# Keys and queries with the dimensions in rows, values by units and weights by chunks: a layout change of the inputs in a fused attention and feed-forward kernel

## The chip, the core and the metric

The kernel runs on one core of one Trainium2 chip, in float32. The metric is device time in microseconds (us) of one launch. Five engines work side by side: PE (TensorE, matmuls), DVE (VectorE), ACT (ScalarE), POOL (GpSimd) and SP (SyncE, which here only issues DMAs). PE reads its operands from SBUF, on-chip memory of 128 partitions, and writes its results to PSUM, from where ACT or DVE must fetch them. Inputs lie in HBM and are brought to SBUF by 16 DMA engines that all queues share.

## The reference

For 2 batches of 8 heads, 768 positions and 64 dimensions: attention of each query over the keys less than 16 positions away, and over 24 summary keys (the maximum of each block of 32 keys) with the mean values of those blocks; then two feed-forward layers on the 1536 resulting rows of 512.

```python
k_sum = k.reshape(B, H, nb, 32, D).max(axis=3)
v_sum = v.reshape(B, H, nb, 32, D).mean(axis=3)
scores_l = np.where(abs(pos_q - pos_k) < 16, scale * q @ k.T, -1e9)
scores_s = scale * q @ k_sum.T + np.log(32)
a = softmax(concat[scores_l, scores_s])
x = a @ concat[v, v_sum]                       # then rows of 512: 8 heads x 64
x = (silu(x @ w_gate) * (x @ w_val)) @ w_out   # 512 -> 1536 -> 512
h = x @ w_in                                   # 512 -> 2048
out = (h * clip(h + 3, 0, 6) / 6) @ w_out2     # 2048 -> 512
```

The feed-forward weights come as 64-bit floats and are turned into pairs of 32-bit parts on the chip (`weights`, L360): four DVE instructions on the bits, one or two on ACT, and a subtraction.

## The kernel before

The 1536 rows are cut into four token blocks t of 384 (two for each batch b), the eight heads into four pairs c. `attention` (L790) adds, for one block, the work of its four pairs: `keys` and `values` for the first block of a batch, then `queries`, `scores`, `sums`, `norm`, `head`, `outputs`.

A matmul contracts over partitions. For the scores it needs keys and queries with the 2 x 64 dimensions of a pair in the partitions, but the inputs have positions in rows. So `load_rows` (L551) brings 128 positions to the partitions, 64 floats (256 bytes) at a time, `rows` (L590) turns them with three transposing matmuls against the identity (L592), and `put` copies the result out of PSUM into `kT` or `qT` (`copy`, L271, so that the trace shows L273, L275 or L277). The query's copy multiplies by -1/8. For batch 0 the rows lie in room of the later tiles x2 and x3 (`stage`, L558; tiles named early in the trace), for batch 1 in rings of four (`kn`) and two (`qn`). There is one `kT` for each pair, used by both batches in turn, with 16 positions of zeros at either end. `ksum` is the maximum of each 32 columns of `kT` (L621).

`scores` (L677) multiplies 64 queries with the 24 summary keys and with a window of 96 keys (L697). `sums` (L709) adds the mask and takes the negated maximum in one DVE instruction (L717), then ACT exponentiates (L724). `head` (L741) divides by the sum on POOL or DVE and transposes the weights (L754), `outputs` (L760) multiplies them with `vw`, a tile with 24 rows of mean values and a window of 96 values for each of the block's six units of 64 queries (L768). The windows overlap, and `load_vw` (L577) fetches them in three DMAs for each pair and block, from rows of 64 floats; it must wait until the weighting of the block before has read the tile.

The feed-forward part takes three matmuls (L334 to L336) for each product of split numbers. Its first group of columns is woven with the attention of the later blocks. Weights of `w_gate`, `w_val` and `w_in` are fetched by columns in pieces of 128 64-bit numbers (1 KB), those of the two output matrices in rows of 4 KB (`w_src`, L353).

A planner (`Plan`, L94 to L255) sets the order of all engines' queues: each step is added with a rank and an assumed time for each engine that could do it; the planner runs the steps through a model of the engines and rings, six times with new ranks, and keeps the best order. All loads count as one engine "dma" there and, but for the second pair's first keys and queries (ACT's queue, `second`, L565), are issued by SP in that order. Where the plan leaves PE idle, `fill` puts up to ten matmuls of zeros (L835).

Of the kernel before, what the change touches and what calls it, by code (L numbers as in the profile page):

```python
# [34 lines left out]
NEG = 1.0e9  # L35

# [23 lines left out]
def consts():  # L60

    import numpy as np

    a = np.zeros((P, P + 3 * NK + NS), np.float32)
    a[:, :P] = np.eye(P, dtype=np.float32)
    i = (np.arange(P) % QB)[:, None]
    second = (np.arange(P) >= QB)[:, None]
    w = np.arange(NW)[None, :]
    near = np.abs(i - (w - HALO)) < WIN
    for n in range(3):  # L70
        m = a[:, P + n * NK : P + (n + 1) * NK]
        inside = second | (w >= HALO) if n == 0 else ~second | (w < QB + HALO) if n == 2 else (w >= 0)
        m[:, :NS] = -np.log(np.float32(BLOCK))
        m[:, NS:] = np.where(near & inside, 0.0, NEG)
    p = np.arange(WP)
    a[p, P + 3 * NK + p * (S // WP) // BLOCK] = 1.0 / BLOCK
    return a

# [180 lines left out]
def tile_kernel(ctx: ExitStack, tc: tile.TileContext, q, k, v, w_gate, w_val, w_out1, w_in2, w_out2, cst, out):  # L259
# [30 lines left out]
    for n in ("kn", "qn", "v3", "qT", "p", "st", "pt"):  # L290
        pools[n] = ab_p
# [61 lines left out]
    def w_src(layer, i, f):  # L353
        if layer == 0 and i < 2 or layer == 1 and i == 0:
            w = ((w_gate, w_val), (w_in2,))[layer][i]
            return w[:, f * P : (f + 1) * P].bitcast(U32).rearrange("(c p) f -> p c f", p=P)
        w = (w_out1, w_out2)[layer]
        return w[f * P : (f + 1) * P, :].bitcast(U32)

    def weights(rank, layer, g, i, f, after):  # L360
# [4 lines left out]
        def load():  # L365
            src = w_src(layer, i, g * (G1, G2)[layer] + f)
            dst = new(raw, [P, 512, 2], U32).rearrange("p a b -> p (a b)")
            if len(src.shape) == 3:
                dst = dst.rearrange("p (c f) -> p c f", c=KC)
            nc.sync.dma_start(out=dst, in_=src)  # L370
# [175 lines left out]
    kT = [ap_.tile([P, S + 2 * HALO], F32, name=f"kT{c}") for c in range(NP)]  # L546
    vw = [ap_.tile([P, NB, P], F32, name=f"vw{c}") for c in range(NP)]
# [3 lines left out]
    def load_rows(dst, src, queue=nc.sync):  # L551

        for h in range(2):
            queue.dma_start(out=dst[:, :, h * D : (h + 1) * D], in_=src[h].rearrange("(r p) d -> p r d", p=P))

    early = {}

    def stage(kind, c, part):  # L558

        x = 3 if kind == "k" else 2  # L560
        if x not in early:
            early[x] = xpool.tile([P, 8, TR, P], F32, tag=f"x{x}", name=f"early{x}")
        return early[x][:, 2 * c + part]
# [13 lines left out]
    def load_vw(t, c):  # L577
        b, s0 = divmod(t * T, S)
        va = v[b, 2 * c]
        end, cut0, cut1 = (0, HALO, NW) if s0 == 0 else (NB - 1, 0, QB + HALO)  # L580
        inner = 1 if s0 == 0 else 0
        first = s0 + end * QB - HALO + cut0
        src = bass.AP(va.tensor, va.offset + first * D, [[D, cut1 - cut0], [S * D, 2], [1, D]])
        nc.sync.dma_start(out=vw[c][NS + cut0 : NS + cut1, end, :].rearrange("p (h d) -> p h d", h=2), in_=src)
        for h in range(2):
            first = h * S + s0 + inner * QB - HALO
            src = bass.AP(va.tensor, va.offset + first * D, [[D, NW], [QB * D, NB - 1], [1, D]])
            nc.sync.dma_start(out=vw[c][NS : NS + NW, inner : inner + NB - 1, h * D : (h + 1) * D], in_=src)

    def rows(ps, src):  # L590
        for r in range(TR):
            nc.tensor.transpose(ps[:, r, :], src[:, r, :], ident)  # L592

    def keys(rank, b, c):

        for part in range(2):
            n = ("kn" if b else "k0", b, c, part)

            def load(n=n, part=part):
                if b == 0:  # L600
                    tiles[n] = stage("k", c, part)
                else:
                    new(n, [P, TR, P])
                load_rows(tiles[n], k[b, 2 * c : 2 * c + 2, part * T : (part + 1) * T], second(b, c))

            add(rank - LEAD["k_load"], {"dma": 1.05}, load, w=[n])
            ps = prep_bank(b, "k", b, c, part)

            def turn(n=n, ps=ps):
                tiles[ps] = new_bank(ps, [P, TR, P])  # L610
                rows(tiles[ps], tiles[n])

            def put(e, part=part, ps=ps):
                dst = kT[c][:, HALO + part * T : HALO + (part + 1) * T].rearrange("q (r p) -> q r p", p=P)
                copy(e, dst, tiles[ps])

            add(rank, {"pe": 0.3}, turn, r=[n, ("cs",)], w=[ps, ("kT", c)])
            add(rank - LEAD["k_put"], {"act": 0.4, "dve": 0.47}, put, r=[ps], w=[("kT", c)])

        def most():  # L620
            nc.vector.tensor_reduce(  # L621
                ksum[c], kT[c][:, HALO : HALO + S].rearrange("q (n i) -> q n i", i=BLOCK), AX.X, ALU.max
            )

        add(rank, {"dve": 0.87}, most, r=[("kT", c)], w=[("ksum", c)])
# [27 lines left out]
    def queries(rank, t, c):  # L653
        n, ps, qt = ("qn" if t > 1 else "q0", t, c), prep_bank(t, "q", t, c), ("qT", t, c)
        b, s0 = divmod(t * T, S)

        def load():
            if t < 2:
                tiles[n] = stage("q", c, t)
            else:  # L660
                new(n, [P, TR, P])
            load_rows(tiles[n], q[b, 2 * c : 2 * c + 2, s0 : s0 + T], second(t, c))

        add(rank - LEAD["q_load"], {"dma": 1.05}, load, w=[n])

        def turn():
            tiles[ps] = new_bank(ps, [P, TR, P])
            new(qt, [P, TR, P])
            rows(tiles[ps], tiles[n])

        def put(e):
            copy(e, tiles[qt], tiles[ps], -1.0 / float(D) ** 0.5)

        add(rank, {"pe": 0.3}, turn, r=[n, ("cs",)], w=[ps, qt])
        add(rank - LEAD["q_put"], {"act": 0.4, "dve": 0.47}, put, r=[ps], w=[qt])

    def scores(rank, t, c):  # L677

        half, qt = t % 2, ("qT", t, c)
        names = [(t, c, h) for h in range(2)]  # L680

        def go(j):
            if j == 0:
                new(("st", t, c), [P, 4, 2 * TR])
            for x in names:
                if j == 0:
                    tiles["at", "s", *x] = new_bank(("at", "s", *x), [P, TR, NK])
                    new(("p", *x), [P, TR, NK])
            q2 = tiles[qt].rearrange("q r p -> q (r p)")
            for far in (True, False):  # L690
                for a in range(2):
                    for h in range(2):
                        hs, u = slice(h * D, (h + 1) * D), 2 * j + a
                        k0 = half * T + u * QB
                        rhs = ksum[c][hs, :] if far else kT[c][hs, k0 : k0 + NW]
                        cols = slice(0, NS) if far else slice(NS, NK)
                        nc.tensor.matmul(  # L697
                            tiles["at", "s", *names[h]][a * QB : (a + 1) * QB, j, cols],
                            lhsT=q2[hs, u * QB : (u + 1) * QB], rhs=rhs, start=True, stop=True,
                        )  # L700

        for j in range(TR):
            add(rank, {"pe": 0.37}, lambda j=j: go(j), r=[("kT", c), ("ksum", c), qt],
                w=[("st", t, c)] + [(n, *m, *x) for x in names for n, *m in (("at", "s"), ("p",))] if j == 0 else
                [("at", "s", *x) for x in names])
# [3 lines left out]
    def sums(rank, t, c, h):  # L709
# [5 lines left out]
        def top(r):  # L715
# [3 lines left out]
                scale=1.0, scalar=3.0e38, op0=ALU.add, op1=ALU.min, accum_out=tiles[st][:, 0, h * TR + r : h * TR + r + 1],  # L719
# [94 lines left out]
    def clear():  # L814
        for c in range(NP):
            nc.gpsimd.memset(kT[c][:, :HALO], 0.0)
            nc.gpsimd.memset(kT[c][:, HALO + S :], 0.0)
        for c in range(NP):
            nc.gpsimd.memset(vw[c], 0.0)

    add(-50.0, {"pool": 3.2}, clear, w=[(n, c) for c in range(NP) for n in ("kT", "vw", "vs")])
# [93 lines left out]
_INS = ["q", "k", "v", "moe_w_gate", "moe_w_val", "moe_w_out", "moe2_w_in", "moe2_w_out"]  # L915
# [20 lines left out]
```

## Time and profile before

| | |
|---|---|
| median of three runs | 653.56 us (653.07 to 653.57) |
| profiled execution | 654.63 us, span 652.9 us |
| PE busy | 640.2 us of the span |
| DVE, ACT, POOL busy | 438.3, 289.7, 52.9 us |
| DMA packets | 73319, of them 45744 under 512 bytes |

The span runs from the first to the last instruction of the profiled execution. A PE that is busy may be at work on fill matmuls, so its share alone says nothing of useful work. Rows of the trace give a start, a duration, the engine, the line and what is written from what.

### The profile page before, as it was taken

Reading aid. Unit: us, or ns where it says so; the run is one execution under the profiler, and the core shown is the slowest. Engines: PE = TensorE matmul, PEld = TensorE weight load, DVE = VectorE, ACT = ScalarE, POOL = GpSimd, SP = SyncE. Lnnn points to the kernel's source line nnn. Section 1 sums busy time; section 2 is a strip of 40 time slices with the busy share of each in tenths; the row PEclk is TensorE's granted clock in tenths of the full one; section 3 lists DMA queues with packets and bytes.
Section 4 is the critical chain, followed back from the end, with each engine's and each line's share of the span. In section 5 each row is a group of like instructions: output and inputs, shape, how many; then the busy total and the mean of one; then the engine's idle time right before and its main releaser. Section 6 shows DMA issues by size and latency. Waiting matters only on the chain.

```text
span 652.9 us, 11688 instructions
## 1 busy us (share of the span) xinstructions
PE 640.2 (98%) x4576; PEld 601.1 (92%) x4576; DVE 438.3 (67%) x972; ACT 289.7 (44%) x674; POOL 52.9 (8%) x73
## 2 busy tenths in 40 slices
PE   7799999999999999999999999999999999999997
PEld 6688888999999999999999999999999999999996
DVE  3789974589997978369754997286738753333332
ACT  3788788455543433134322564354424332222220
POOL 3435443100000000000000000000000000000000
PEclk9989999999999999999999999999999999999999
DMA  8998944043433233003210133012301000000112
GB/s 185 220 225 232 193 85 140 1 130 132 159 130 98 97 97 97 1 27 103 81 50 0 66 103 124 1 65 64 131 1 40 25 1 0 2 1 0 50 49 96
DMA packets 73319, 53.84 MB, mean 82 GB/s; under 512 B 45744, under 2 KB 66736, under 8 KB 73264
## 3 DMA queue, kind: packets, MB, share of 16 engines
q1 hardware_dynamic: 70864, 52.51, 28.7%
q10 hardware_dynamic: 2400, 0.59, 0.6%
q8 instruction: 36, 0.59, 0.4%
q14 instruction: 19, 0.16, 0.1%
HBM read 49.94 MB, written 3.15 MB: 81 GB/s over the span
## 4 chain that ended last, share of the span: by engine, by line
PE 92%; DMA 4%; ACT 2%; issue 0%; SPq 0%; DVE 0%; POOL 0%; ACTq 0%; POOLq 0%
PE mm L334 16%; PE mm L335 15%; PE mm L336 15%; PE mmb L334 13%; PE mmb L335 13%; PE mmb L336 13%; PE at_s L697 2%; PE pv L768 2%; DMA vn<-in_v 2%; DMA early<-in_k 1%; PE at_t L754 1%; ACT p L724 1%; DMA kn<-in_k 1%; PE pv L835 1%; PE at_q L592 1%
## 5 line engine op out<-in xcount | busy, mean ns | idle before, releaser
L334 PE MATMUL mm<-x,wa 128*128 128x384 f32 x196 | 69.2, 353 | 0.0
L336 PE MATMUL mm<-x,wa 128*128 128x384 f32 x196 | 65.9, 336 | 0.0
L335 PE MATMUL mm<-x,wa 128*128 128x384 f32 x196 | 65.9, 336 | 0.0
L387 ACT ACTIVATE raw<-raw 128x512 f32<-128x512 f32 x68 | 46.2, 680 | 26.3 <-DVE bits L379 23.4
L335 PE MATMUL mmb<-x,wb 128*128 128x384 f32 x160 | 53.5, 335 | 0.0
L335 PE MATMUL mm<-x,wb 128*128 128x384 f32 x160 | 53.5, 335 | 0.0
L336 PE MATMUL mmb<-x,wb 128*128 128x384 f32 x160 | 53.5, 334 | 0.0
L336 PE MATMUL mm<-x,wb 128*128 128x384 f32 x160 | 53.5, 334 | 0.0
L334 PE MATMUL mm<-x,wb 128*128 128x384 f32 x160 | 53.5, 334 | 0.0
L334 PE MATMUL mmb<-x,wb 128*128 128x384 f32 x160 | 53.5, 334 | 0.0
L273 ACT ACTIVATE g<-u 128x384 fp32r<-128x384 f32 x61 | 32.0, 525 | 43.5 <-DVE u L431 22.6
L391 DVE SCALAR_TENSOR_TENSOR bits<-raw,bits 128x512 f32<-128x512 f32 x68 | 46.6, 685 | 1.1 <-ACT raw L387 0.6
L379 DVE SCALAR_TENSOR_TENSOR bits<-raw,bits 128x512 uint32<-128x512 uint32 x68 | 46.9, 690 | 0.4
L383 DVE SCALAR_TENSOR_TENSOR bits<-raw,bits 128x512 uint32<-128x512 uint32 x68 | 46.9, 690 | 0.1
L280 DVE TENSOR_TENSOR g<-u,g 128x384 fp32r<-128x384 f32 x59 | 33.5, 568 | 19.2 <-ACT g L273 19.1
L273 ACT ACTIVATE gb<-u 128x384 fp32r<-128x384 f32 x51 | 26.8, 525 | 37.4 <-DVE u L431 19.2
L724 ACT ACTIVATE p<-p,st 128x120 f32<-128x120 f32 x96 | 36.9, 388 | 10.5 <-DVE st L717 10.5
L335 PE MATMUL mmb<-x,wa 128*128 128x384 f32 x124 | 41.5, 335 | 0.0
L336 PE MATMUL mmb<-x,wa 128*128 128x384 f32 x124 | 41.5, 334 | 0.0
L334 PE MATMUL mmb<-x,wa 128*128 128x384 f32 x124 | 41.5, 334 | 0.0
L273 ACT ACTIVATE wb<-bits 128x512 fp32r<-128x512 f32 x33 | 20.9, 633 | 44.6 <-DVE bits L391 16.9
L280 DVE TENSOR_TENSOR gb<-u,gb 128x384 fp32r<-128x384 f32 x51 | 28.3, 555 | 16.7 <-ACT gb L273 16.6
(198 smaller groups left out, 1659.9 us busy)
## 6 DMA issues: line engine op xcount, KB each, us to landing
raw<-in_moe_w_out SPq DMA_DIRECT2D x28, 512.0 KB, 3.2
raw<-in_moe_w_in SPq DMA_DIRECT2D x16, 512.0 KB, 3.7
raw<-in_moe_w_gate SPq DMA_DIRECT2D x12, 512.0 KB, 4.2
raw<-in_moe_w_val SPq DMA_DIRECT2D x12, 512.0 KB, 3.6
vw<-in_v SPq DMA_DIRECT2D x32, 120.0 KB, 3.6
vn<-in_v SPq DMA_DIRECT2D x8, 384.0 KB, 4.6
out<-oacc SPq DMA_DIRECT2D x11, 256.0 KB, 2.0
kn<-in_k SPq DMA_DIRECT2D x16, 96.0 KB, 4.7
```

The lines of the kernel that those rows point to most:

```text
L273: nc.scalar.activation(dst, src, AF.Copy, scale=scale)
L280: eng[e].tensor_tensor(dst, a, b, ALU.subtract)
L334: nc.tensor.matmul(ps, lhsT=lh, rhs=rh, start=j == 0, stop=False)
L335: nc.tensor.matmul(ps, lhsT=ll, rhs=rh, start=False, stop=False)
L336: nc.tensor.matmul(ps, lhsT=lh, rhs=rl, start=False, stop=j == n_k - 1)
L379: nc.vector.scalar_tensor_tensor(t, high_w(), 0xC0000000, t, ALU.bitwise_and, ALU.bitwise_or)
L383: nc.vector.scalar_tensor_tensor(t, low_w(), 29, t, ALU.logical_shift_right, ALU.bitwise_or)
L387: nc.scalar.activation(mag, mag, AF.Abs)
L391: nc.vector.scalar_tensor_tensor(as_f(), mag, 2.0**-15, as_f(), ALU.is_ge, ALU.mult)
L697: nc.tensor.matmul(tiles["at", "s", *names[h]][a * QB : (a + 1) * QB, j, cols], lhsT=q2[hs, u * QB : (u + 1) * QB], rhs=rhs, start=True, s ...
L724: nc.scalar.activation(a, a, AF.Exp, bias=s[:, 0, n : n + 1], scale=-1.0, accum_out=s[:, 1, n : n + 1])
L768: nc.tensor.matmul(tiles[pv][h * D : (h + 1) * D, u * QB : (u + 1) * QB], lhsT=vw[c][:NK, u, h * D : (h + 1) * D], rhs=tiles[pts[h]][:, u ...
```

## The change

All inputs but the values keep their content and get another order in HBM before the launch. Keys and queries come as [batch, pair, 2 x 64 dimensions, positions], keys with 16 zeros at either end. The values come a second time (`vu`) as [batch, pair, 64 positions of a unit, units, 2 x 64], with a unit of zeros at either end. The three weights that were read by columns come as [block of 128 columns, partition, chunk, column], so that a partition's part is 4 KB in one run.

With that, transposes and their copies are gone; `kT` and the queries' tile are loaded as they are used. Batch 0's first three `kT` lie in the room of x3, batch 0's queries in that of x2, and batch 1 has `kT` tiles of its own. The scale -1/8 moves into L717, the masks are divided by it. A key load is one DMA of 400 KB for a pair and batch (four of 96 KB before), a query load one of 192 KB (two of 96 before). A window load stays three DMAs: 64 rows, and two of 16 rows for the overlap with the units beside. The planner's times for loads are lowered, the other leads and ranks stay.

```diff
+    if name in ("q", "k"):
+        a = a.reshape(B, NP, 2, S, D).transpose(0, 1, 2, 4, 3).reshape(B, NP, P, S)
+        if name == "k":
+            a = np.pad(a, ((0, 0), (0, 0), (0, 0), (HALO, HALO)))
+    elif name == "vu":
+        a = a.reshape(B, NP, 2, S // QB, QB, D).transpose(0, 1, 4, 3, 2, 5).reshape(B, NP, QB, S // QB, P)
+        a = np.pad(a, ((0, 0), (0, 0), (0, 0), (1, 1), (0, 0)))
+    elif name in ("moe_w_gate", "moe_w_val", "moe2_w_in"):
+        a = a.reshape(KC, P, -1, P).transpose(2, 1, 0, 3)
...
-                 kn=4, qn=2, v3=1, qT=2, p=4, st=2, pt=4)
+                 v3=1, qT=4, p=4, st=2, pt=4)
...
-            return w[:, f * P : (f + 1) * P].bitcast(U32).rearrange("(c p) f -> p c f", p=P)
+            return w[f].bitcast(U32).rearrange("p c f -> p (c f)")
...
+    early_k = xpool.tile([P, NP - 1, S + 2 * HALO], F32, tag="x3", name="early_k")
+    early_q = xpool.tile([P, 2, NP, T], F32, tag="x2", name="early_q")
+    kT = {(b, c): ap_.tile([P, S + 2 * HALO], F32, name=f"kT{b}_{c}") if b or c == NP - 1 else early_k[:, c]
+          for b in range(B) for c in range(NP)}
...
+        u0, to = half * NB, vw[c]
+        nc.sync.dma_start(out=to[NS + HALO : NS + HALO + QB], in_=vu[b, c, :, u0 + 1 : u0 + 1 + NB])
+        nc.sync.dma_start(out=to[NS : NS + HALO], in_=vu[b, c, QB - HALO :, u0 : u0 + NB])
+        nc.sync.dma_start(out=to[NS + HALO + QB :], in_=vu[b, c, :HALO, u0 + 2 : u0 + 2 + NB])
...
+            second(2 * b, c).dma_start(out=kT[b, c], in_=k[b, c])
...
-            add(rank, {"pe": 0.3}, turn, r=[n, ("cs",)], w=[ps, ("kT", c)])
-            add(rank - LEAD["k_put"], {"act": 0.4, "dve": 0.47}, put, r=[ps], w=[("kT", c)])
...
+        add(rank - LEAD["k_load"], {"dma": 1.35}, load, w=[n])
...
-        add(rank, {"pe": 0.3}, turn, r=[n, ("cs",)], w=[ps, qt])
-        add(rank - LEAD["q_put"], {"act": 0.4, "dve": 0.47}, put, r=[ps], w=[qt])
+            second(t, c).dma_start(out=tiles[n], in_=q[b, c, :, half * T : (half + 1) * T])
+
+        add(rank - LEAD["q_load"], {"dma": 0.68}, load, w=[n])
...
-                scale=1.0, scalar=3.0e38, op0=ALU.add, op1=ALU.min, accum_out=tiles[st][:, 0, h * TR + r : h * TR + r + 1],
+                scale=-SCALE, scalar=3.0e38, op0=ALU.add, op1=ALU.min, accum_out=tiles[st][:, 0, h * TR + r : h * TR + r + 1],
...
-            add(r - LEAD["vw_load"], {"dma": 1.75}, lambda c=c: load_vw(t, c), w=[("vw", c)])
+            add(r - LEAD["vw_load"], {"dma": 1.1}, lambda c=c: load_vw(t, c), w=[("vw", c)])
```

The zeroing of `kT`'s ends and of `vw` on POOL (`clear`, L814) goes too.

## Rows read from the trace of the kernel before

**Rows 1.** The page, part 1: busy us, share of the span, instructions
```profile
PE 640.2 (98%) x4576; PEld 601.1 (92%) x4576; DVE 438.3 (67%) x972; ACT 289.7 (44%) x674; POOL 52.9 (8%) x73
```

**Rows 2.** By stretch: length, busy us of each engine, PEclk, DMA share, GB/s
```profile
30.00:37.00 7.00, 5.31 (x50) 4.21 (x49) 6.86 (x25) 6.06 (x20) 5.09 (x5) 0.76 1.13 230
37.00:60.00 23.00, 22.66 (x362) 19.93 (x362) 20.51 (x80) 20.68 (x74) 7.99 (x9) 1.00 0.89 220
60.00:90.00 30.00, 29.22 (x364) 25.53 (x363) 28.07 (x81) 22.45 (x67) 15.74 (x18) 1.00 0.85 172
90.00:126.00 36.00, 36.00 (x560) 32.13 (x559) 17.88 (x91) 27.32 (x98) 9.74 (x12) 1.00 0.30 81
126.00:200.00 74.00, 74.00 (x429) 74.00 (x428) 70.58 (x134) 39.64 (x72) 0.00 (x0) 1.00 0.40 128
```

**Rows 3.** The chain that ended last, in order of time: start us, us, what
```profile
36.24 0.32 PE mm L334
...
122.53 0.85 PE pv L768 x24
```

**Rows 4.** By stretch, fill matmuls (L835) alone: length, PE, PEld, PEclk, DMA
```profile
0.00:37.00 37.00, 11.91 (x126) 10.35 (x126) 0.95 0.98 209
```

**Rows 5.** By stretch, transposes of keys and queries (L592) alone
```profile
37.00:126.00 89.00, 9.46 (x57) 6.73 (x57) 1.00 0.64 148
60.00:90.00 30.00, 5.39 (x33) 3.95 (x33) 1.00 0.85 172
```

**Rows 6.** Timeline of PE from 60 to 82 us: start us, us, engine, line
```profile
69.78 0.34 PE L336 MATMUL mm<-x,wa 128*128 128x384 f32 x1
...
70.46 0.33 PE L335 MATMUL mm<-x,wa 128*128 128x384 f32 x1
```

**Rows 7.** Waits of PE from 37 to 126 us: total us, times, longest
```profile
PE at_k L592 <- ACT kT L273: 0.8, 1, 0.8
```

**Rows 8.** Groups on DVE, 37 to 126 us: busy us, mean ns, idle before
```profile
L275 DVE TENSOR_SCALAR qT<-at_q 128x384 f32<-128x384 f32 x3 | 1.7, 555 | 1.1 <-PE at_q L592 1.1
L277 DVE COPY kT<-at_k 128x384 f32<-128x384 f32 x2 | 1.1, 542 | 0.0
```

**Rows 9.** DMA from 60 to 90 us: packets, MB, share of 16 engines
```profile
DMA packets 14625, 5.17 MB, mean 172 GB/s; under 512 B 13916, under 2 KB 13916, under 8 KB 14620
...
q1 hardware_dynamic: 14620, 5.11, 84.2%
```

**Rows 10.** DMA from 466 to 505 us, loads of 4 KB rows alone
```profile
q1 hardware_dynamic: 432, 1.57, 11.2%
```

**Rows 11.** Timeline from 0 to 40 us: start us, us, engine, line
```profile
1.18 2.01 SPq L554 DMA_DIRECT2D early<-in_k  x4
...
5.32 0.45 SPq L812 DMA_DIRECT2D cs<-in_cst  x1
...
10.48 0.31 PE L697 MATMUL at_s<-ksum,qT 64*64 64x24 f32 x8 [1.80 <-ACT qT L273]
...
11.61 0.28 DVE L717 CUSTOM_DVE_ANT_0 p<-at_s,cs 128x120 f32<-128x120 f32 x1 [1.09 <-PE at_s L697]
...
22.56 0.31 PE L697 MATMUL at_s<-ksum,qT 64*64 64x24 f32 x8
...
26.67 0.31 PE L697 MATMUL at_s<-ksum,qT 64*64 64x24 f32 x8
```

**Rows 12.** DMA issues: count, KB each, median us from issue to landing
```profile
raw<-in_moe_w_out SPq DMA_DIRECT2D x28, 512.0 KB, 3.2
...
vw<-in_v SPq DMA_DIRECT2D x32, 120.0 KB, 3.6
...
vw<-in_v SPq DMA_DIRECT2D x16, 40.0 KB, 3.9
...
cs<-in_cst SPq DMA_DIRECT2D x1, 192.0 KB, 4.7
```

**Rows 13.** Waits of SP's DMA queue, whole span: total us, times, longest
```profile
SPq L584 <- PE pv L768: 12.1, 5, 5.5
```

More of the change, by code (lines that the diff above doesn't have):

```diff
@@ L35 @@
 NEG = 1.0e9
+SCALE = 1.0 / D**0.5
 LEAD = dict(
@@ L72, in consts @@
         inside = second | (w >= HALO) if n == 0 else ~second | (w < QB + HALO) if n == 2 else (w >= 0)
-        m[:, :NS] = -np.log(np.float32(BLOCK))
-        m[:, NS:] = np.where(near & inside, 0.0, NEG)
+        m[:, :NS] = np.log(np.float32(BLOCK)) / SCALE
+        m[:, NS:] = np.where(near & inside, 0.0, -NEG / SCALE)
     p = np.arange(WP)
@@ L543, in out2 @@
             add(rank, {"dma": 0.73 * n / DM}, store, r=[("o", t, m)])
-    kT = [ap_.tile([P, S + 2 * HALO], F32, name=f"kT{c}") for c in range(NP)]
-    vw = [ap_.tile([P, NB, P], F32, name=f"vw{c}") for c in range(NP)]
+    vw = [ap_.tile([NK, NB, P], F32, name=f"vw{c}") for c in range(NP)]
     ksum = [ap_.tile([P, NS], F32, name=f"ksum{c}") for c in range(NP)]
     vn = {}
[L551 to L563, printed above, removed]
+    early_k = xpool.tile([P, NP - 1, S + 2 * HALO], F32, tag="x3", name="early_k")
+    early_q = xpool.tile([P, 2, NP, T], F32, tag="x2", name="early_q")
+    kT = {(b, c): ap_.tile([P, S + 2 * HALO], F32, name=f"kT{b}_{c}") if b or c == NP - 1 else early_k[:, c]
+          for b in range(B) for c in range(NP)}
     def second(t, c):
@@ L577, in load_vw @@
     def load_vw(t, c):
[L578 to L588, printed above, removed]
@@ L590, in rows @@
-    def rows(ps, src):
-        for r in range(TR):
-            nc.tensor.transpose(ps[:, r, :], src[:, r, :], ident)
-    def keys(rank, b, c):
[L596 to L615, printed above, removed]
-            add(rank, {"pe": 0.3}, turn, r=[n, ("cs",)], w=[ps, ("kT", c)])
-            add(rank - LEAD["k_put"], {"act": 0.4, "dve": 0.47}, put, r=[ps], w=[("kT", c)])
+        b, half = divmod(t, 2)
@@ L623, in most @@
             )
-        add(rank, {"dve": 0.87}, most, r=[("kT", c)], w=[("ksum", c)])
+        add(rank - LEAD["k_load"], {"dma": 1.35}, load, w=[n])
+        add(rank, {"dve": 0.87}, most, r=[n], w=[("ksum", c)])
     def values(rank, b, c):
@@ L653, in queries @@
     def queries(rank, t, c):
-        n, ps, qt = ("qn" if t > 1 else "q0", t, c), prep_bank(t, "q", t, c), ("qT", t, c)
-        b, s0 = divmod(t * T, S)
+        n = ("qT" if t > 1 else "q0", t, c)
+        b, half = divmod(t, 2)
         def load():
             if t < 2:
-                tiles[n] = stage("q", c, t)
+                tiles[n] = early_q[:, t, c]
             else:
[L661 to L672, printed above, removed]
-        add(rank, {"pe": 0.3}, turn, r=[n, ("cs",)], w=[ps, qt])
-        add(rank - LEAD["q_put"], {"act": 0.4, "dve": 0.47}, put, r=[ps], w=[qt])
+                new(n, [P, T])
+            second(t, c).dma_start(out=tiles[n], in_=q[b, c, :, half * T : (half + 1) * T])
+        add(rank - LEAD["q_load"], {"dma": 0.68}, load, w=[n])
     def scores(rank, t, c):
-        half, qt = t % 2, ("qT", t, c)
+        b, half, qt = t // 2, t % 2, ("qT" if t > 1 else "q0", t, c)
         names = [(t, c, h) for h in range(2)]
```

31 lines of the change are left out of this document (13 added, 18 removed).

## The prediction

> **What bounds the kernel now.** I read the engines first, then busy time by stretch, then the chain that ended last, then what fills PE and what it waits for. PE is busy for 98% of the span, no other engine for more than 67% [rows 1]. But the run has three parts to be kept apart. Until the first matmul of the feed-forward part, at 36.24 us [rows 3], PE mostly turns zeros: 126 fill matmuls, 11.9 us [rows 4]. What is full there is the DMA, with a share over 1 from 30 to 37 us, and still 0.89 and 0.85 in the next two stretches [rows 2]. From 37 us to the last weighting of values at 122.5 us [rows 3], attention for token blocks 1 to 3 is woven into the first feed-forward group; PE is busy 22.7 of 23, 29.2 of 30 and 36 of 36 us [rows 2] and its longest wait is 0.8 us [rows 7], so PE sets the pace. DVE is close behind from 37 to 90: 20.5 of 23 and 28.1 of 30 us [rows 2]. After that no attention is left and nothing that the change touches is on the path, except that the loads of three of the five weights get runs of 4 KB in place of 1 KB. I cost that at nothing: the raw ring loads each weight while earlier ones are converted and multiplied. Were that cover gone, PE would wait for a load, 3.2 us [rows 12], at each of the later seven weight groups; that it doesn't now shows from 126 to 200 us, where PE is busy 74 of 74 us [rows 2].
>
> **Transposes of keys and queries: -6.3 us.** 96 matmuls of L592 go, in groups of three. 57 of them, 19 groups, lie after 37 us [rows 5]; the other 39 lie before, where PE has fill to spare. The price of a group is what it adds to PE's stream. Matmuls of L334 to L336 start 0.173 us apart; the two that start at 69.78 and 70.46 [rows 6] are two such steps and one group apart, so a group costs 0.68 - 2 x 0.173 = 0.33 us. 19 x 0.33 = 6.3 us, all on the path because PE sets the pace there.
>
> **Their evictions: -0.8 us of waits, and room elsewhere.** The 32 copies out of PSUM go, 0.54 to 0.56 us each on DVE [rows 8], and ACT has most of them. The only wait of PE that they cause after 37 us is 0.8 us, for a put of kT [rows 7]; it goes. The scale moves from the query's eviction into L717, whose instruction has a scale operand already and keeps its 128x120 shape: zero, between -0.02 and +0.02 us for each of 96.
>
> **DVE as the next limit: +0.9 us.** Between 60 and 90 us PE sheds 11 groups (33 transposes [rows 5]), 3.7 us, and the wait, so the stretch would be 25.5 us long. DVE has 28.07 us there [rows 2] and sheds two kT copies and one of three qT copies [rows 8], 1.6 us: 26.4. The difference, 0.9 us, is given back; it is zero if the planner pulls weight conversion forward, and 3.7 if nothing moves.
>
> **DMA before the first matmul: -7.7 us.** 16 loads of 96 KB for keys, 16 for queries of blocks 0 and 1, and 12 for windows of values (4 of 40, 8 of 120 KB) run in pieces of 256 B: 16,770 packets. From 60 to 90 us the queue is busy 84.2% with 13,916 such packets and 1.55 MB in longer ones [rows 9]. The longer ones cost 16 engines x 39 us x 11.2% = 70 engine-us per 1.57 MB, by a stretch of 4 KB rows [rows 10]; that leaves 404 - 69 = 335 engine-us, 24 ns a packet. So these loads hold all 16 engines for 16,770 x 24 ns / 16 = 25 of the 36 us. In runs of 1.5 to 3.2 KB the same 4.3 MB take 12 us at the 359 GB/s of those 4 KB rows. So 13 us is the most that can be won here; the least is nothing, if the chain of attention itself takes as long.
>
> What I take comes from that chain. Scores of the head pairs of block 0 begin at 10.48 us, (the second pair between), 22.56 and 26.67 us [rows 11]: 12.1 us for two steps and 4.1 for the last, the one whose loads had long been issued. With 4.1 for each: 12.3 in place of 16.2, -3.9. The first pair: its key load, issued at about 1.2 us [rows 11], lands within 3.2 us (the 512 KB row [rows 12]), no copy follows, and DVE's first maximum is then held by the masks. Those are 192 KB and take 4.7 us to landing [rows 12]; they are issued at 5.32 now, behind eight loads at half a us each, and at about 3.1 us behind four: landed at 7.8, against 11.61 for the first maximum now [rows 11], -3.8. Together -7.7, and the first feed-forward matmul near 28.5 us. Inside this lies that ACT issues two loads of the second pair in place of six, and isn't held from its work by them.
>
> **Windows of values.** Three DMAs per pair and block, before and after, but 192 and twice 48 KB in place of 40 and twice 120, the small ones over 16 partitions. A 40 KB piece takes 3.9 us to landing and a 120 KB one 3.6 [rows 12]: the size of a piece doesn't set it, so I cost the new ones at nothing, between -0.3 and +0.3 us each, beside the scores of the same pair. One rule speaks against it: the Trainium skill, "DMA: Bandwidth & Descriptors", section Rules for kernel authors, says that transfers under 64 KB pay mostly overhead and should be one large one. By the fixed cost that this page gives, about 2 us, two small pieces for each of 16 pairs would be 64 us if paid in series, an estimate from that page. The rows speak for overlap, and the sum keeps zero. The 12 memsets of POOL at the start go too, and nothing but a fill matmul waited for them.
>
> **The sum.** 6.3 + 0.8 - 0.9 + 7.7 = 13.9 us. The profiled execution took 654.63 us, its span 652.9: 640.7. The runs' median is 653.56, 1.1 us below it: 639.7 us.
>
> **Rivals.**
> A. The DMA is full, but it isn't what the first matmul waits for: exponentials, conversion of the first weight and POOL's weighing take as long as before, and the 7.7 don't come. 653.56 - 6.2 = 647.4. For it: DVE has 6.9 of 7 us from 30 to 37 [rows 2]. Against it: long steps where loads were late, 4.1 where they weren't. That longer runs don't move faster than short ones ends here too.
> B. The whole 13 us of DMA time come off and DVE's work moves forward with them: 6.3 + 0.8 + 13 = 20.1, 633.5 us. For it: copies and issues that held ACT and DVE go as well. Against it: the last step shows 4.1 us a pair without late loads.
> C. Slower: the small pieces of the windows become the pace of SP's queue, each landing before the next counts. Four pairs x (3.6 + 2 x 3.9) = 46 us before the last pair of block 0 can be weighted, with 9.6 us behind it as now from the last scores to the first matmul (26.67 to 36.24) gives 56, 19 to 20 us later: 653.6 + 19.5 - 6.2 = 667 us. It decides from the point where serial landings add over 6.2 us. Against it: 48 window loads at 3.7 us would be 178 us in series [rows 12], but all are in by 122.5 [rows 3]. It is what the skill's rule on small transfers would come to here.
> D. DVE becomes the bound over 37 to 90 us: its 48.6 us less 1.6, with the 4.4 us of gaps that it has now, are 51.4 in place of 53, and a faster start only makes PE wait for converted weights. SP, too, already waits 12.1 us for pv before it may overwrite a window [rows 13], with the group's weights queued behind. Then 1.6 us are left: 652.0.
>
> **How the numbers follow.** Forecast (636 to 644.5) 0.58, A 0.20, B 0.12, D 0.05, C 0.05. Without C, the half of D and the ends of A and B, 632.5 to 648.5 holds about 8 in 10. A change of 0.2%, 1.3 us, is about what a measurement can tell from none. Faster by more: 0.58 + 0.20 + 0.12 and a little of D, 0.91; the same 0.03; slower 0.06.
>
> **What would show it.** Scores of the first pair start near 6 to 7 us and DVE's first maximum stands near 8; the four starts are 4 us apart; the first matmul of L334 stands near 28.5 us; the DMA share up to there is clearly under 1; the last weighting, now at 122.5, comes near 109; PE's steps from there to the end are as before. If the first matmul stays past 34 us, A holds; if PE shows idle time with DVE as releaser up to 90 us, D; if pv waits for window loads, C. The forecast is wrong most easily in the 7.7, the difference of two starts that the trace doesn't show.

## The result, and the profile after

The changed kernel takes 647.12 us, the median of four runs from 645.35 to 647.15, beside 653.52 us for the kernel before (653.07 to 653.57). The ratio is 0.990, with a 95% interval of 0.988 to 0.991: 6.4 us faster where 13.9 were forecast. The profiled execution took 647.14 us, its span 645.0. That of before was 1.1 us above its median, so the two traces differ by 7.9 us of span, and the account below is of these 7.9.

The page of the changed kernel, part 1 (busy us, share of the span, instructions), answers [rows 1].

```profile
PE 629.9 (98%) x4477; PEld 589.5 (91%) x4477; DVE 436.9 (68%) x970; ACT 277.8 (43%) x646; POOL 45.2 (7%) x59
```

PE is busy for 10.3 us less and the span is 7.9 us shorter: PE stands still for 2.4 us longer than before. By stretch (length, busy us of each engine, PEclk, DMA share, GB/s), beside [rows 2]:

```profile
7.00:16.00 9.00, 6.49 (x128) 4.98 (x124) 6.09 (x30) 4.93 (x21) 3.71 (x6) 0.81 1.06 292
...
0.00:37.00 37.00, 28.46 (x540) 22.85 (x540) 25.01 (x97) 21.49 (x77) 13.70 (x22) 0.95 0.90 250
37.00:60.00 23.00, 19.96 (x336) 16.18 (x330) 22.07 (x82) 19.52 (x71) 10.51 (x12) 1.00 0.94 271
60.00:90.00 30.00, 30.00 (x388) 26.12 (x387) 27.06 (x88) 21.42 (x67) 12.01 (x15) 1.00 0.42 116
90.00:126.00 36.00, 36.00 (x432) 32.97 (x431) 18.85 (x77) 22.61 (x79) 6.41 (x8) 1.00 0.20 73
126.00:200.00 74.00, 74.00 (x428) 74.00 (x428) 70.39 (x132) 37.56 (x68) 0.00 (x0) 1.00 0.39 136
```

From 37 to 60 us PE is busy 20.0 of 23 us, against 22.7 before; from 60 us on it is full. The start was expected to leave the DMA with air. Instead it moved 250 GB/s over the first 37 us where it had moved 209 [rows 4], and its share is over 1 from 7 to 16 us: room that the short packets left was taken at once by loads that had stood behind them. PE's timeline from 6 to 32 us (start us, us, engine, line) answers [rows 11]:

```profile
6.82 0.31 PE L666 MATMUL at_s<-ksum,early_q 64*64 64x24 f32 x8 [1.12 <-DVE ksum L601]
...
10.96 0.29 PE L666 MATMUL at_s<-ksum,early_q 64*64 64x24 f32 x2
...
16.70 0.31 PE L666 MATMUL at_s<-ksum,early_q 64*64 64x24 f32 x8
...
21.46 0.33 PE L666 MATMUL at_s<-ksum,early_q 64*64 64x24 f32 x8
...
31.11 0.44 PE L354 MATMUL mm<-x,wa 128*128 128x384 f32 x1
```

The four pairs' scores start at 6.8, 11.0, 16.7 and 21.5 us, steps of 4.1, 5.7 and 4.8, and the first feed-forward matmul at 31.1. In before's trace the first of these starts at 35.89, just ahead of the one in the chain [rows 3], and the first transposes of keys at 6.29:

```profile
6.29 0.50 PE L592 MATMUL mm_k<-cs,early 128*128 128x128 f32 x3
...
35.89 0.67 PE L334 MATMUL mm<-x,wa 128*128 128x384 f32 x1
```

The chain that ended last, from its beginning to its last weighting, says what the start hangs on now:

```profile
1.19 4.60 DMA early_k<-in_k
5.81 8.23 DMA vw<-in_vu
...
14.89 9.14 DMA vn<-in_v
...
26.32 0.57 DVE bits L401
...
36.29 0.87 PE pv L737 x24
...
39.27 3.99 DMA kT<-in_k
43.28 0.95 DVE ksum L601
...
113.68 0.85 PE pv L737 x24
```

Loads carry it up to 24 us. One of them is a load of values for the block means (vn), which the change doesn't touch, and it takes 9.14 us from issue to landing. From 24 to 59 us the chain runs on DVE, but for the stretch from 35.2 to 43.3: there it goes over scores and a weighting on PE, three window loads that SP issues once that weighting is done, and a load of keys that stands behind them in SP's queue. The issues by kind (count, KB each, median us to landing):

```profile
vn<-in_v SPq DMA_DIRECT2D x8, 384.0 KB, 7.5
vw<-in_vu SPq DMA_DIRECT2D x16, 192.0 KB, 5.2
...
kT<-in_k SPq DMA_DIRECT2D x5, 400.0 KB, 8.1
vw<-in_vu SPq DMA_DIRECT2D x32, 48.0 KB, 4.7
...
cs<-in_cst SPq DMA_DIRECT2D x1, 192.0 KB, 7.0
```

The masks landed in 4.7 us before [rows 12], and the same vn loads in 4.6:

```profile
vn<-in_v SPq DMA_DIRECT2D x8, 384.0 KB, 4.6
```

PE's waits from 31 to 60 us (total us, times, longest), where before had 1.1 us in all from 37 to 126, 0.8 of it in [rows 7]:

```profile
PE at_t L723 <- POOL p L717: 1.1, 3, 0.6
PE at_t L723 <- POOL v L617: 1.1, 1, 1.1
PE mm L356 <- DVE x L300: 0.7, 1, 0.7
PE pv L737 <- DVE x L300: 0.6, 1, 0.6
```

**The account.** The first feed-forward matmul comes 4.8 us earlier, and one unit of scores (1.0 us of PE) is done before it that used to come after. From there to 60 us PE waits longer and turns more zeros: it runs 42 feed-forward matmuls between 37 and 60 us where it ran 56. From the last weighting on (113.68 us, before 122.53 [rows 3]) PE is as full as before, with six feed-forward matmuls more still to do (2859 in place of 2853): 531.3 and 530.4 us to the end of the span. So -4.8 - 1.0 at the start, the transposes, and new waits add up to -7.9. How the last two divide is the second experiment.

### The profile page after: what moved, and what is told of

Its sections match the earlier page's. It is cut to its first block, busy times and chain, and to the rows that moved or that the text cites. A ratio compares the mean times of both kernels' runs of the same rounds, so it can differ in the third digit from the quotient of the medians.

```text
span 645.0 us, 11380 instructions
## 1 busy us (share of the span) xinstructions
PE 629.9 (98%) x4477; PEld 589.5 (91%) x4477; DVE 436.9 (68%) x970; ACT 277.8 (43%) x646; POOL 45.2 (7%) x59
## 4 chain that ended last, share of the span: by engine, by line
PE 90%; DVE 4%; DMA 4%; SPq 0%; issue 0%
PE mm L354 16%; PE mm L356 15%; PE mm L355 15%; PE mmb L356 13%; PE mmb L354 13%; PE mmb L355 13%; DMA vn<-in_v 1%; PE pv L737 1%; DMA vw<-in_vu 1%; PE at_s L666 1%; DVE p L686 1%; PE at_t L723 1%; DMA early_k<-in_k 1%; DVE bits L401 1%; DMA kT<-in_k 1%; DVE bits L409 0%
## 5 line engine op out<-in xcount | busy, mean ns | idle before, releaser
L300 DVE TENSOR_TENSOR gb<-u,gb 128x384 fp32r<-128x384 f32 x51 | 28.3, 555 | 16.7 <-ACT gb L293 16.6
```

What stands on the lines that cost most here:

```text
L300: eng[e].tensor_tensor(dst, a, b, ALU.subtract)
```

## The experiments

All are compared with the kernel before on the same chip (its medians: 653.5 to 654.4 us). The last column is the start of the first feed-forward matmul in the profiled execution.

| kernel | median us | ratio to before, 95% | first matmul |
|---|---|---|---|
| the change | 647.12 | 0.990 (0.988 to 0.991) | 31.1 |
| before_few | 649.23 | 0.993 (0.990 to 0.996) | 32.4 |
| after_few | 643.84 | 0.984 (0.981 to 0.987) | 27.8 |
| before_turns2 | 658.71 | 1.006 (1.004 to 1.008) | 36.6 |
| before_light | 653.49 | 0.999 (0.997 to 1.001) | 35.0 |
| after_light | 645.32 | 0.987 (0.984 to 0.990) | 31.2 |
| after_few_light | 644.79 | 0.984 (0.982 to 0.987) | 32.0 |
| after_masks | 647.27 | 0.990 (0.987 to 0.992) | 30.3 |
| after_onewin | 645.18 | 0.987 (0.984 to 0.991) | 29.7 |
| after_oldvw | 647.52 | 0.990 (0.987 to 0.993) | 30.4 |
| after_oldw | 646.72 | 0.988 (0.984 to 0.991) | 30.4 |
| after_order | 646.98 | 0.989 (0.986 to 0.991) | 32.6 |
| after_order_one | 647.20 | 0.989 (0.987 to 0.991) | 29.7 |
| one_hop | 652.03 | 0.997 (0.995 to 0.999) | 30.1 |
| one_hop_bias | 658.33 | 1.007 (1.005 to 1.009) | 31.4 |

**Did the DMA hold the start?** before_few and after_few leave out three of four key loads of batch 0 and query loads of block 0; the first pair's stand in for them.

```diff
-                load_rows(tiles[n], k[b, 2 * c : 2 * c + 2, part * T : (part + 1) * T], second(b, c))
+                if b or c == 0:
+                    load_rows(tiles[n], k[b, 2 * c : 2 * c + 2, part * T : (part + 1) * T], second(b, c))
...
-                load_rows(tiles[n], q[b, 2 * c : 2 * c + 2, s0 : s0 + T], second(t, c))
+                if t or c == 0:
+                    load_rows(tiles[n], q[b, 2 * c : 2 * c + 2, s0 : s0 + T], second(t, c))
```

> The kernel before with the same loads left out as in the changed kernel's run (three of four key loads of batch 0, three of four query loads of block 0; pairs 1 to 3 work with pair 0's rows, so their results are wrong): 6,912 packets of 256 B, 24 ns each on 16 engines, 10 us of DMA. Nothing else changes, transposes and copies stay. If the DMA held the first feed-forward matmul of the kernel before (the prediction's step), it moves from 36 to 27 to 31 us. If PE then keeps pace as it did after 36 us, the time falls by as much (5 to 8 us, 646 to 649); if DVE, ACT and POOL give it back up to 60 us, as in the changed kernel, by 1 to 4 us, and PE's waits between 31 and 60 us grow to 3 us or more. If the first matmul stays past 34 us, the DMA wasn't what held it.

```diff
-            second(2 * b, c).dma_start(out=kT[b, c], in_=k[b, c])
+            if b or c == 0:
+                second(2 * b, c).dma_start(out=kT[b, c], in_=k[b, c])
...
-            second(t, c).dma_start(out=tiles[n], in_=q[b, c, :, half * T : (half + 1) * T])
+            if t or c == 0:
+                second(t, c).dma_start(out=tiles[n], in_=q[b, c, :, half * T : (half + 1) * T])
```

> The changed kernel with three of the four key loads of batch 0 and three of the four query loads of block 0 left out (pairs 1 to 3 use the keys and queries of pair 0, so their results are wrong): 1.8 MB less of the 9.3 MB that the changed kernel moves in its first 37 us; all other instructions and their order stay. Theory V (loads set the pace of the first 31 us): landings of the rest shorten, the first feed-forward matmul comes 2.5 to 4 us earlier (1.8 MB at 250 to 290 GB/s would be 6 to 7 us of DMA, not all of it on the path), and the time falls by 2 to 4 us. Theory W (DVE up to 60 us gives back what is won): the first matmul may come earlier, but PE's waits between there and 60 us grow by as much, and the time stays within 1 us of the changed kernel's 647.1.

In part, in both. The kernel before starts its first feed-forward matmul 3.5 us earlier and ends 4.6 us earlier; the changed one 3.3 and 3.3. For the kernel before, 32.4 us lies between the 27 to 31 that stood for the prediction's step and the 34 that stood against it. Neither gives a start's gain back. before_few, from 37 to 60 us, keeps PE as busy as before:

```profile
37.00:60.00 23.00, 22.74 (x340) 20.34 (x340) 21.71 (x78) 21.12 (x74) 10.03 (x11) 1.00 0.83 214
```

The changed kernel, with these loads gone, reaches 27.8 us, past the forecast's 28.5. But the prediction had loads lengthen the steps from one pair's scores to the next, and the steps of before_few say otherwise. Its first and its fourth pair's scores start here:

```profile
9.06 0.31 PE L699 MATMUL at_s<-ksum,qT 64*64 64x24 f32 x8 [0.55 <-DVE ksum L622]
...
25.27 0.31 PE L699 MATMUL at_s<-ksum,qT 64*64 64x24 f32 x8
```

That is 16.2 us for the three steps, as in [rows 11] with all the loads. The 3.5 us lie elsewhere: 1.4 ahead of the first scores, 2.1 between the last scores and the first feed-forward matmul. In after_few, without these loads and without transposes, the steps take 13.5 us together (6.17 to 19.64), in the change 14.6.

**What is a group of transposes worth?** before_turns2 does those of batch 1's keys and of blocks 1 to 3's queries twice, 20 groups of three more.

```diff
-    def rows(ps, src):
-        for r in range(TR):
+    def rows(ps, src, times=1):
+        for r in list(range(TR)) * times:
...
-                rows(tiles[ps], tiles[n])
+                rows(tiles[ps], tiles[n], 2 if b else 1)
...
-            rows(tiles[ps], tiles[n])
+            rows(tiles[ps], tiles[n], 2 if t else 1)
```

> The kernel before with the transposes of keys of batch 1 and of queries of blocks 1 to 3 done twice: 20 groups of three more on PE, no more copies or loads, the order of the queues as before. The prediction's term (0.33 us a group, all of it on the path after 36 us) has +6.3 to 6.7 us: 659.8 to 660.3. If PE only looked full there and was in step with another engine, the groups cost less than half: under 656.7.

The medians differ by 4.3 us, the spans by 5.2; the last weighting comes 5.2 later than in [rows 3]:

```profile
127.77 0.85 PE pv L768 x24
```

That is 0.21 to 0.26 us a group, less than the 0.33 forecast and more than half of it. In PE's stream, though, the second group costs as much as the first. The two steps of [rows 6], which take 0.68 us with one group between them, take 1.01 us with two:

```profile
72.28 0.34 PE L336 MATMUL mm<-x,wa 128*128 128x384 f32 x1
...
73.29 0.34 PE L335 MATMUL mm<-x,wa 128*128 128x384 f32 x1
```

What hides a part of it shows between the first feed-forward matmul and the last weighting (length, busy us of each engine, PEclk, DMA share, GB/s). These are before, before_turns2 and after_order, a run further down that gives PE the same matmuls there as before, but for the transposes:

```profile
35.89:122.53 86.64, 85.53 (x1248) 75.30 (x1248) 66.14 (x248) 69.97 (x236) 34.58 (x40) 0.99 0.67 155
36.57:127.77 91.20, 90.92 (x1306) 81.16 (x1306) 65.81 (x249) 70.75 (x236) 34.99 (x40) 1.00 0.61 146
32.61:115.15 82.54, 79.25 (x1189) 69.02 (x1188) 65.06 (x247) 65.26 (x223) 35.51 (x40) 1.00 0.52 160
```

PE's busy time is 5.4 us longer with 19 groups more and 6.3 us shorter with 19 fewer, 0.28 to 0.33 us a group. (The first three steps of before there, at a granted clock of 0.50 from 35.9 to 37.0 us, took 1.11 us where before_turns2 took 0.61; without these 0.5 us both differences come near 5.8, 0.31 a group.) before_turns2 takes only 4.6 us longer there because PE's 1.1 us of waits shrink to 0.3. By that price the new waits in the account come to 3.3 to 4.2 us: -4.8 - 1.0 - 5.4 + 3.3, or -4.8 - 1.0 - 6.3 + 4.2. Counted from the first feed-forward matmul on, PE in the changed kernel stands still for 3.9 us up to 60 us and turns 1.3 us of zeros; before it was 1.1 and 0.7 us in the whole stretch. That is 3.4 us more.

**Is DVE the new limit?** after_light and before_light leave out two of DVE's steps on each weight of the first group, 18 instructions of some 0.7 us.

```diff
+            if (layer, g) == (0, 0):
+                return
```

> The kernel before with the same 18 DVE instructions left out. Theory W: before the change PE set the pace after 36 us, so only what the first weight's conversion holds up before the first feed-forward matmul (two weights, some 1.4 to 2.8 us of DVE) can come off: 651 to 653.5. Theory V: nothing comes off, 653 to 653.6. If it falls by as much as the changed kernel does (4 us or more), DVE was a limit before the change too and its role isn't what sets the two kernels apart.

> The changed kernel without two of the four DVE instructions on the bits of each of the nine weights of the first group (the sign and the guard, 18 instructions of about 0.7 us, 12.6 us of DVE), so the weights of that group are wrong; the order of all queues is that of the changed kernel. Theory W (from 24 to 60 us DVE is the limit of the changed kernel and gives back what PE sheds): the first feed-forward matmul, now at 31.1 us, comes 1 to 3 us earlier, PE's waits between 31 and 60 us go, and the time falls by 4 to 7 us, to 640 to 643. Theory V (the loads set the pace, DVE only waits with them): DVE gets idle time with loads as releaser, and the time falls by less than 1.5 us, to 645.6 or more.

> Both at once: the missing key and query loads, and without the sign and guard instructions of the first weight group on DVE (which alone gave 645.3, -1.8). If loads and DVE are two limits of the same stretch, one behind the other, the two together give clearly more than the sum of both alone: 640 to 643. If each is a small cost of its own they add up (about 644.5 where the loads alone give -1). If neither matters much because the order of PE's queue holds it in step with the chain of attention (scores, maximum, exponential, weighing on POOL, transposes, weighted values), then about 645, as with DVE alone.

In the kernel before it changes nothing (0.999), so DVE didn't hold it. In the changed one 1.8 us come, between the two theories (4 to 7, and under 1.5), and hardly clear of noise: the intervals of after_light and of the change overlap. From 37 to 60 us DVE falls from 22.1 to 18.8 us, but PE gets only from 20.0 to 20.1:

```profile
37.00:60.00 23.00, 20.12 (x353) 17.07 (x352) 18.79 (x74) 19.51 (x70) 9.83 (x12) 1.00 0.93 268
```

So DVE alone isn't it, though the chain of the changed kernel runs on it there. In after_light the chain goes mostly over PE from 25 us on, and again over a load of keys that stands behind window loads in SP's queue (issued at 37.9 us, landed at 41.7). No run moved that load, so what it costs stays open. Nor did relieving DVE add to fewer loads: after_few_light (644.8) stands at after_few's 643.8. Its profiled execution had a granted clock of 0.75 and 0.59 in stretches of the start, which leaves its first matmul at 32.0, so it says little on the start.

**The masks.** The forecast's first pair hung on their landing. after_masks issues them first, on ACT's queue.

```diff
-        nc.sync.dma_start(out=cs[:, P:], in_=cst[:, P:])
+        nc.scalar.dma_start(out=cs[:, P:], in_=cst[:, P:])
...
-    add(MASKS, {"dma": 0.55}, masks, w=[("masks",)])
+    add(-95.0, {"dma": 0.55}, masks, w=[("masks",)])
```

> The changed kernel with the load of the masks moved from SP's fifth place to ACT's queue, as its first; the planner orders the rest anew. In the changed kernel the masks are issued at 3.2 us and take 7.0 to landing, and DVE's first maximum stands at 10.76 in place of the 7.8 that the prediction had. If the masks hold it, it moves to 8 to 8.7 us (scores of the first pair end at 7.8) and theory V has the first feed-forward matmul 1.5 to 2.5 us earlier and the time 1.5 to 3 us lower, 644 to 645.6. Theory W: the first maximum comes earlier but DVE's work up to 60 us is the same, so the time falls by less than 1 us.

They land within 2.7 us of their issue, yet DVE's first maximum starts at 9.62 instead of 10.76, and the time is the same. DVE in the changed kernel, from 8 to 11 us, shows why:

```profile
8.27 0.69 DVE L617 TENSOR_TENSOR vn<-vn 96x512 f32<-96x512 f32 x1 [1.50 <-DMA vn<-in_v]
8.88 0.94 DVE L601 TENSOR_REDUCE ksum<-early_k 128x24 f32<-128x768 f32 x1
9.91 0.92 DVE L617 TENSOR_TENSOR vn<-vn 96x512 f32<-96x512 f32 x1
10.76 0.27 DVE L686 CUSTOM_DVE_ANT_0 p<-at_s,cs 128x120 f32<-128x120 f32 x1
```

A step that waits for vn stands ahead of the maximum on DVE; with the masks early that step, and vn's landing, hold it. In after_masks it is the instruction just before the maximum:

```profile
9.01 0.69 DVE L617 TENSOR_TENSOR vn<-vn 96x512 f32<-96x512 f32 x1 [2.88 <-DMA vn<-in_v]
```

**The windows and the weights.** after_onewin loads each window as one piece of 288 KB over 96 rows, after_oldvw as before, in 256 B runs; after_oldw loads the weights in 1 KB runs as before.

```diff
-        nc.sync.dma_start(out=to[NS + HALO : NS + HALO + QB], in_=vu[b, c, :, u0 + 1 : u0 + 1 + NB])
-        nc.sync.dma_start(out=to[NS : NS + HALO], in_=vu[b, c, QB - HALO :, u0 : u0 + NB])
-        nc.sync.dma_start(out=to[NS + HALO + QB :], in_=vu[b, c, :HALO, u0 + 2 : u0 + 2 + NB])
+        nc.sync.dma_start(out=to[NS:], in_=vu[b, c, :, u0 : u0 + NB])
```

> The changed kernel with each window of values loaded by one DMA of 96 rows of 3 KB (288 KB) in place of one of 64 and two of 16 rows; for that the values are laid out in HBM with the overlaps repeated. If the small pieces slow the queue (rival C of the prediction in a mild form, and a part of theory V): landings of the neighbours (values 7.5 us, keys 8.1) fall by a third or more and the time falls by 1 to 3 us. If landings are long because the DMA engines are simply full (theory V without the pieces) or don't matter (theory W): within 0.7 us of the changed kernel, 646.4 to 647.8.

> The changed kernel with the windows of values loaded as before, from rows of 64 floats (40 and twice 120 KB in runs of 256 B) with the tile zeroed by POOL first; the planner's times stay those of the changed kernel. Theory V by the price of a packet (1,120 packets of 24 ns on 16 engines, 1.7 us a window, for 0.8 to 0.9 in long runs): 3 to 4 us more DMA before the first feed-forward matmul, time 648.5 to 650.5. If the 16-row pieces cost the DMA as much as the short runs did (the run with one piece was 1.9 us faster than the changed kernel): 646 to 648. Theory W: 646.5 to 648.

```diff
-            return w[f].bitcast(U32).rearrange("p c f -> p (c f)")
+            return w[:, f * P : (f + 1) * P].bitcast(U32).rearrange("(c p) f -> p c f", p=P)
```

> The changed kernel with the three weights read by columns in runs of 1 KB as before. The prediction costed this part at nothing after the start. In the first 31 us three such loads take 1.6 to 1.7 us of DMA each in place of 1.5: theory V 0 to +1 us on the first matmul; all theories: within 1 us of 647.1, and from 126 us on PE as before.

The old windows (647.5) and the old weights (646.7) give the changed kernel's time: neither part is worth anything that these runs can tell, and the 3 to 4 us more of DMA that the price of a packet asked for with the old windows didn't come. One piece gives 645.2, 1.9 us less than the change, with intervals that overlap; the landings of vn and kT shorten to:

```profile
vw<-in_vu SPq DMA_DIRECT2D x16, 288.0 KB, 5.5
vn<-in_v SPq DMA_DIRECT2D x8, 384.0 KB, 6.5
kT<-in_k SPq DMA_DIRECT2D x5, 400.0 KB, 6.9
```

**The order of the queues.** The planner orders DVE's instructions otherwise once the steps are gone: 238 of 967 stand elsewhere. after_order puts the change's work and loads into before's order, by empty steps that cost the planner what the old ones did; after_order_one adds the one-piece window.

```diff
+            ps = prep_bank(b, "k", b, c, part)
+
+            def turn():
+                pass
+
+            def put(e):
+                pass
+
+            add(rank, {"pe": 0.3}, turn, r=[n, ("cs",)], w=[ps, ("kT", c)])
+            add(rank - LEAD["k_put"], {"act": 0.4, "dve": 0.47}, put, r=[ps], w=[("kT", c)])
```

> The changed kernel's work in the order of the kernel before: the planner is given the old steps, times and rings (transposes, copies, two loads for each half), and where the program is written out the transposes, their copies and the second loads are simply not there; the loads are those of the changed kernel. The order on DVE, ACT and POOL is then that of the kernel before, where the changed kernel has 238 of its 967 DVE instructions in other places. Theory S (the planner's new order gives back the gain: PE waits 4 us more after the first feed-forward matmul): PE's waits from there to 60 us stay under 1.5 us and the time is 640 to 643.5. Theory W (DVE, ACT and POOL are full up to 60 us whatever the order): PE is busy 20 to 20.5 of 23 us from 37 to 60 as in the changed kernel, and the time is 645.5 to 648.

> The same order of before, with one 96-row load for each window of values in place of three. Theory S with the small pieces as a cost of their own (they were worth 1.9 us in the changed kernel's order): 638.5 to 642. If the 1.9 us came from another order or timing by chance rather than from the pieces: within 0.7 us of the run before.

after_order by stretch, and PE's longest wait after 31 us:

```profile
7.00:16.00 9.00, 6.78 (x133) 5.15 (x132) 4.23 (x21) 3.76 (x14) 4.32 (x6) 0.77 1.06 301
16.00:23.00 7.00, 6.76 (x85) 4.58 (x83) 3.98 (x22) 4.68 (x17) 2.71 (x4) 0.50 1.04 278
23.00:31.00 8.00, 7.14 (x104) 5.85 (x104) 6.62 (x28) 6.30 (x27) 3.27 (x4) 0.63 0.61 193
...
37.00:60.00 23.00, 22.14 (x329) 19.50 (x330) 22.29 (x79) 20.37 (x70) 10.09 (x11) 1.00 0.71 228
60.00:90.00 30.00, 28.10 (x385) 24.23 (x384) 25.87 (x85) 21.48 (x68) 14.98 (x17) 1.00 0.56 153
```

```profile
PE at_t L747 <- POOL p L741: 1.9, 2, 1.7
```

In that order PE is busy 22.1 of 23 us from 37 to 60 and does 60 feed-forward matmuls there, where the change does 42, with DVE as full as in the change: the order makes the waits there. But 1.9 us stand still from 60 to 90, the first feed-forward matmul comes 1.5 us later, at a granted clock of 0.50 to 0.77, and the total is the same 647.0, so neither theory came whole. From the first feed-forward matmul to the end it takes 612.9 us, the change 613.9 with a unit of scores (1.0 us) less to do: by these two traces about 2.0 us of the new waits are the order's. The 1.9 us of the one-piece window don't come in this order (647.2 against 647.0), so I don't count them as shown for the window by itself.

Two more put the planner's clock closer to the landings measured: a DMA's result counted 5.0 us later in place of 2.6 (one_hop), and DVE's bias at 0.8 in place of 0.4 as well (one_hop_bias), both with the one-piece window.

```diff
-    HOP = {"pe": 0.12, "act": 0.12, "dve": 0.14, "pool": 0.14, "dma": 2.6, "none": 0.0}
+    HOP = {"pe": 0.12, "act": 0.12, "dve": 0.14, "pool": 0.14, "dma": 5.0, "none": 0.0}
```

> The kernel with one 96-row load per window (645.2 us alone), planned with 5.0 us from a load to its reader in place of 2.6, since loads of the changed kernel took 4.4 to 8.1 us to landing in the first 40 us and the planner ordered the queues for shorter ones. If the order of the queues is part of the loss: PE's waits between the first feed-forward matmul and 60 us fall below 1.5 us and the time to 641 to 644. If DVE, ACT and POOL are simply full there: 644.5 to 646.

> As the run before, and the planner's penalty for choosing DVE where ACT or POOL could do a step raised from 0.4 to 0.8 us. If DVE's share of the copies and subtractions holds PE up to 60 us (theory W), DVE's busy time from 37 to 60 us falls below 21.5 us and the time by another 0.5 to 2 us, 640 to 643.5; if not, as the run before or slower, since POOL takes 1.3 us for what DVE does in 0.5 to 0.6.

They end 6.9 and 13.2 us above after_onewin, where 641 to 646 us was expected of one_hop. It has the same steps on the same loads, with some seven more of them on POOL; one_hop_bias moves far more from DVE to POOL. In one_hop PE has waits of 2.9 and 2.3 us, and the stretch behind them is at a lower granted clock:

```profile
PE at_v L622 <- DVE st L685: 2.9, 1, 2.9
PE mm L355 <- ACT wa L294: 2.3, 1, 2.3
```

```profile
60.00:90.00 30.00, 26.59 (x305) 22.70 (x306) 24.10 (x78) 20.18 (x63) 11.60 (x14) 0.83 0.35 99
```

## Why the prediction was wrong, step by step

The sign and the parts from which the gain comes were right, and the wide range (632.5 to 648.5) held the time; the forecast's own (636 to 644.5) didn't, and the size, 13.9 us, was more than twice what came. The account gives 7.9 between the traces, 6.0 short: about 1.9 at the start, 0 to 0.9 in the transposes, 3.2 to 4.1 in waits. The other 1.5 lies in the pair: 1.1 between before's profiled execution and its median, 0.4 outside the spans.

- **DMA before the first matmul, -7.7: -4.8 and 1.0 of scores came, in part by another way.** The first scores start at 6.82 us, as marked (6 to 7). But of the 3.7 us by which they come earlier, at most 0.5 are loads: the first keys landed at 5.79 where before turned its first at 6.29, and the transposes and copies that followed in before, up to 10.48, are gone. The failed step is "with 4.1 for each": the steps are 14.6 us together, not 12.3, 1.5 less than before in place of 3.9. The reading behind it, that the two long steps were those whose loads were late, doesn't hold: without these loads before_few has the same 16.2 us of steps. What sets their length wasn't taken apart. The first maximum at 7.8 failed too (10.76), by the landing of the masks (7.0 us, not 4.7) and by vn's step ahead of it: a landing read in the trace of before was taken to hold for the queue after the change. The loads as a whole do hold a part of the start, 3.5 and 3.3 us by before_few and after_few; these runs leave out loads that the pairs wait for as well as loads in others' way, and don't tell the two apart. The mark "DMA share clearly under 1" failed as well: 0.90 over the first 37 us, over 1 from 7 to 16.
- **Transposes, -6.3: right, 5.4 to 6.3.** The price of 0.33 us was read at one place, and the doubled groups cost it again. "All on the path" holds for PE's own time. But between 37 and 60 us PE no longer sets the pace in the changed kernel, and waits take the place of what it sheds.
- **The wait for a put of kT, -0.8: gone as said, and outweighed.** No wait of that kind is left, but 3.5 us of others stand from 31 to 60 us.
- **DVE as the next limit, +0.9: wrong place and too small.** This is the larger of the two failed steps: that "PE sets the pace" from 37 us on was kept for the changed kernel, and DVE was priced from 60 to 90 us alone. From 60 to 90 us PE is full, and nothing is given back. Before 60, where the prediction put nothing, 3.3 to 4.2 us are. DVE carries the chain there, but no engine alone accounts for them: relieving DVE gave 1.8 us, hardly clear of noise, and left PE's busy time there nearly as it was, and before's order of the queues took most of the waits before 60 us away and let another come behind. In part they turn on the order in which work stands in the queues while DVE (22.1 of 23 us) and ACT (19.5) have little room; which single step sets them stays open.
- **Windows and weights at nothing: right for the old forms against the new.** One piece in place of three won 1.9 us in one order, hardly clear of noise, and nothing in the other. The rule of the Trainium skill ("DMA: Bandwidth & Descriptors", section Rules for kernel authors) that small transfers pay mostly overhead isn't borne out at the 64 us in series that were estimated from it: 1.9 us is the most that these runs show. The fixed cost of about 2 us in that estimate is fitted on that page of the Trainium skill to DMAs issued by GpSimd; the ones here are issued by SP.
- **Rivals.** A gave 647.4 and the time is 647.1, but by another way: its mark, a first matmul past 34 us, didn't come. That the numbers meet is luck. Of D a part came: a chain on DVE and waits on DVE's and POOL's results before 60 us. C didn't come: no wait of PE from 31 to 60 us is for a window, though at 14.05 us SP's queue stood until a window load had landed (8.23 us, in the chain). B didn't either.
- **The last weighting** was to come near 109; it stands at 113.7, and PE's steps behind it are as before, six feed-forward matmuls more.

## What to carry over

When a change frees the DMA ahead of a start, the loads queued behind move up and landings lengthen: price the first waits with the landings of a full queue, not with those in the trace of before. A long step whose loads came late isn't yet a step that the loads made long: leave the loads out and see whether it shortens, before the change is priced by it. An instruction taken from a full engine is worth its price only where that engine stays full after the change, so the stretches have to be forecast again, not only the sum. Doubling the instruction measures the price if it is read in the engine's busy time; the total can hide a part of it in waits that shrink. And where a planner writes the queues, taking steps out reorders the rest, so part of any result is the new order's: nearly the same work took 645 us in one order and 652 in another, there with longer waits and a lower granted clock behind them.

## What the runs showed of the hardware

- An unchanged load, 384 KB, landed in 4.6 us (median of 8) before and in 7.5 after, with 250 in place of 209 GB/s moved in the first 37 us; one took 9.14 us. The masks took 7.0 us in the full queue and 2.7 when issued first.
- PE's granted clock falls in some stretches of the start, and not in the same ones: 0.76 from 30 to 37 us before [rows 2], 0.81 from 7 to 16 in the change, and 0.50, which is the lower level (1.2 GHz), from 16 to 23 in after_order. There PE had been busy 6.78 of 9 us just before; before_few stayed at 1.00 up to 60 us. What sets it wasn't tested, and it adds to the uncertainty of every start compared here.
- A group of three transposes between feed-forward matmuls of PE's stream adds 0.33 us, and a second group right behind it 0.33 more (0.68 and 1.01 us between the same two matmuls, of which 0.35 are theirs).
